# A spectral block on one core: a room of its own for the scaled sum, products of zeros in the first sequence, later weight conversions, and a later first inverse run

## Chip, cores and metric

One Trainium2 chip, one core of it. The metric is the device time of one launch, in microseconds: the median over runs, lower is better. Engines are named as in the profile: PE (TensorE, matmuls), PEld (its weight loads), DVE (VectorE), ACT (ScalarE), POOL (GpSimd), SP (SyncE, which issues all the DMAs here).

## What is computed

For 8 sequences x of 3136 rows and 256 columns, in fp32:

```python
X = rfft(x, axis=1)                          # attention part
Yr = Xr @ w_r - Xi @ w_i + b_r               # complex product, bias
Yi = Xr @ w_i + Xi @ w_r + b_i
Y  = softshrink(Yr, 0.01) + 1j * softshrink(Yi, 0.01)
y  = irfft(Y, n=3136, axis=1)

mixed = real(fft(fft(y, axis=1), axis=2))    # MLP part
u  = y + mixed
un = (u - mean(u)) / sqrt(var(u) + 1e-6)     # over the 256 columns
out = u + relu(un @ w_ch1) @ w_ch2           # 256 -> 1024 -> 256
```

## The kernel before

The 3136-point transform is split as 64 x 49. Each sequence b goes through three phases.

Phase 1 (p1) is the 64-point forward step (fwd tables, tile g_f1), folded by DVE and stored to DRAM (ad; for the first sequence four pieces aq, one per quarter). Phase 2 runs in four quarters q of eight frequencies u. p2_f2 loads af from DRAM, does the 49-point step in two bursts s (tile g_f2 in PSUM, L574) and copies the spectrum X out. p2_w multiplies by the weights wr, ws, wd (tile g_w; L637 for b = 0 with plain fp32, L178 with three products of split fp32 for the others), copies the common term to ks (L646), adds bias and shrinks on DVE (y, m, Y, L651 to L654). For q = 0 POOL builds yz, the first transposing step's input (L663, L664). p2_mix does the transform over the columns (g_mix, four steps per quarter) and stores md. p2_yt transposes Y (g_yt, four steps per quarter) and p2_g2 does the inverse 49-point step in two bursts (g_g2, L812), evicts it by ACT into bev tiles (L817) and stores them to bd (L820). Phase 3: p3_norm loads bf from bd and mt from md, does the inverse 64-point step (tile g_g1, quarters, L442), adds both into ut and takes the statistics; p3_tr transposes ut; p3_mlp1 and p3_mlp2 are the MLP in groups of up to four row blocks, h (L178) to hh and hl (L955, L956), then o (L178) over eight pieces f. At a group's end DVE makes t and a second product from the two o banks and rb, the inverse deviations (L987), adds them to total (L990) and stores the result.

The order is planned: each task is a generator that yields the time at which its next piece is due, in units of one sequence (T), a heap takes the earliest, and a scheduler orders each engine's instructions from that program order. An extra edge can be given by hand: issue_after(x) keeps instructions behind x on its engine, and after(key) holds a generator until another one has set the key. `late` in load_consts and weights is such an edge: the conversion comes behind the ks copy of quarter q of the first sequence, ks_in[0, q]. burst and quarters keep a run of small products together: ACT first copies two elements into the bank (the "held" copies, L443 and L461), so that the run starts when its last input is there.

SBUF tiles share rooms by tag, each with its number of buffers. What the change touches:

```python
# L295, L296: 128x512 zeros for keep_busy, in a buffer of "hl" (3)
# L816, L986: both in "bev", 2 buffers
bev = sb.tile([128, 512], F32, tag="bf" if odd else "bev", bufs=4 if odd else 2, name="bev")
t = rb if k else sb.tile([128, 512], F32, tag="bev", bufs=2, name="t")
# L912: first inverse run of b = 0, also behind the last product w_in[1, 0]
if b == 0 and ms[0] == 0:
    yield from after(("w", 1, 0))
```

keep_busy (L299) multiplies zeros on PE, 35 times behind the first forward step and 8 times behind the first quarter's weights. split_double (L189) turns the MLP weights, which arrive as 64-bit floats, into two fp32r halves: one ACT copy (L203), five DVE instructions (L204 to L212), for w1 also the subtraction of the column mean with two products on PE (L217, L218) and one DVE instruction (L220), then a cast on ACT (L222) and two DVE instructions (L223, L224). weights (L1009) does that in eight parts; the parts of w1 go two at a time. In PSUM there are four banks g, two h and two o.

Of the kernel before, what the change touches and what calls it, by code (L numbers as in the profile page):

```python
# [62 lines left out]
def tables():  # L63
# [26 lines left out]
    for u in range(U):  # L90
# [13 lines left out]
        else:  # L104
# [24 lines left out]
ROOMS = (("m", 1, 400), ("y1", 2, 400), ("eo", 2, 400), ("ks", 2, 400), ("xx", 2, 400),  # L129
         ("W0", 1, 2048), ("W1", 1, 2048), ("W2", 1, 2048), ("W3", 1, 2048), ("mq", 2, 2048),  # L130
         ("uth", 2, 1024), ("utl", 2, 1024), ("tot", 2, 1024), ("af", 2, 1024), ("mt", 2, 1024),
# [3 lines left out]
T = 10000  # L135
# [14 lines left out]
def spectral_block(ctx: ExitStack, tc: tile.TileContext, x, w_ri, b_ri, w1, w2,  # L150
# [89 lines left out]
    def load_consts():  # L240
        yield 0.97 * T
        w_v = w_ri.rearrange("a (k p) e -> a p k e", p=128)
        for name, tag in (("wr", "hh"), ("ws", "hh"), ("wd", "hl")):
            KF[name] = sb.tile([128, 2, D], F32, tag=tag, bufs=3, name=name + "f")
        behind("a0", out=KF["wr"], in_=w_v[0])
        wi = sb.tile([128, 2, D], F32, tag="mt", bufs=2, name="wi")
        behind("a0", out=wi, in_=w_v[1])

        for name, sign in (("ws", -1.0), ("wd", 1.0)):
            va.scalar_tensor_tensor(KF[name], wi, sign, KF["wr"], op0=ALU.mult, op1=ALU.subtract)  # L250
        yield 1.01 * T
        KF["cs"] = sb.tile([128, 2, 129], F32, tag="hl", bufs=3, name="csf")
        behind(1, out=KF["cs"], in_=c_cs)
        behind(1, out=fwd_f, in_=c_fwd)
        yield 1.6 * T
        nc.sync.dma_start(out=inv_f, in_=c_inv)
        late = ks_in[0, 2]
        for name in ("wr", "ws", "wd"):
            with tc.issue_after(late):
                split(name, KF[name])  # L260
            lo_v(K[name][1], KF[name], K[name][0])
        cs = K["cs"] = cp.tile([128, 2, 2, 128], F32R, name="cs")
        t = KF["cs"]
        with tc.issue_after(late):
            sc.copy(cs[:, :, 0], t[:, :, 0:128])
        lo_v(cs[:, :, 1], t[:, :, 0:128], cs[:, :, 0])
        with tc.issue_after(late):
            sc.copy(cs[:, 0, 1, 0:1], t[:, 0, 128:129])
# [24 lines left out]

    mlp_w = {}
    idle_f = sb.tile([128, 512], F32, tag="bev", bufs=2, name="idle_f")  # L295
    idle = sb.tile([128, 512], F32R, tag="hl", bufs=3, name="idle")  # L296
    va.memset(idle_f, 0.0)
    sc.copy(idle, idle_f)

    def keep_busy(last, n):  # L300

        g = gtile("g_idle")
        with tc.issue_after(last):
            for i in range(n):
                te.matmul(g, idle[:, :128], idle, start=True, stop=True)


    a_dram, b_dram, m_dram = {}, {}, {}
    af_ld, f2_in = {}, {}
# [148 lines left out]
    def burst(banks, lates, todo):  # L458


        held = [sc.copy(g[0:1, 0:2], late) for g, late in zip(banks, lates)]  # L461
        f, *args = todo[0]
        first = first_of[0] = f(*args).ins
        for h in held:
            tc.add_manual_dep(first, h.ins.name, mybir.DependencyInfo(mybir.DependencyClass.Sync, mybir.DependencyReason.DATA), reason="bank held")
        with tc.high_priority(), tc.issue_after(first):
            for f, *args in todo[1:]:
                f(*args)

    def p1(b):  # L470

# [80 lines left out]
    def p2_f2(b):  # L552


        for q in range(4):
            base, STEP, F2W, W0, WW, M0 = clock2(b, q)
            u0 = 8 * q
            yield base
            yield from after(("a", b, q) if b == 0 else ("a", b))
            if b == 0:  # L560
                X = sb.tile([128, 2, 2, 8, S], F32, tag=("Xh", "Xl")[q % 2], bufs=1, name="X")
                Xs = sb.tile([128, 2, 8, S], F32, tag=("Xsh", "Xsl")[q % 2], bufs=1, name="Xs")
                xt[b, q] = X, Xs
            else:
                xt[b, q] = Xh, Xl, Xsh, Xsl = x_tiles()
            afs, tfs = zip(*[rows_f2(b, q, s) for s in range(2)])

            for s in range(2):
                yield base + STEP * F2W * s / 2

                def one(i, t, k, j):
                    rows = slice(64 * i, 64 * i + N2)
                    first = t * D + k * 128 + j * 64
                    return te.matmul(banks[i][64 * j:64 * j + 64, k * 200 + t * S:k * 200 + t * S + S], afs[s][rows, first:first + 64],  # L574
                                     tfs[s][rows, t], start=True, stop=True)
                banks = [gtile("g_f2") for _ in range(2)]
                burst([banks[1]], [afs[s][64:65, 0:2]], [(one, i, t, k, j) for t in range(4) for k in range(2) for j in range(2) for i in range(2)])
                if b == 0 and q == 0:
                    f2_in[s] = first_of[0]
                    done.add(("f2", s))  # L580
                gv = [g[:, :400].rearrange("p (k t j) -> p k t j", k=2, t=4) for g in banks]

                def place(t, c=None):
                    return (t if c is None else t[:, :, c])[:, :, s::2]

                def evict(outs):
                    for c, o in enumerate(outs):
                        sc.copy(o, gv[c])
                    if q == 0 and s == 0:
                        for c, o in enumerate(outs):  # L590
                            sc.copy(o[:, :, 0, NM:], gv[1 - c][:, :, 0, NM:])
                if b == 0:
                    xv_ = [place(X, c) for c in range(2)]
                    evict(xv_)
                    va.tensor_add(place(Xs), *xv_)
                    continue
                lo_x = lo_v if b == 1 and q == 0 else lo_g
                xs = sb.tile([128, 2, 4, S], F32, tag="xs", bufs=1, name="xs")
                xh, xl = ([place(t, c) for c in range(2)] for t in (Xh, Xl))
                if s == 0:  # L600
                    xx = [sb.tile([128, 2, 4, S], F32, tag="xx", bufs=2, name="xx") for c in range(2)]
                    evict(xx)
                    for c in range(2):
                        sc.copy(xh[c], xx[c])  # L604
                        lo_x(xl[c], xx[c], xh[c])
                    va.tensor_add(xs, *xx)
                else:
                    im = sb.tile([128, 2, 4, S], F32, tag="im", bufs=1, name="im")
                    sc.copy(im, gv[1])
                    sc.copy(xh[0], gv[0])  # L610
                    va.tensor_add(xs, gv[0], im)
                    lo_v(xl[0], gv[0], xh[0])
                    sc.copy(xh[1], im)
                    lo_v(xl[1], im, xh[1])
                sc.copy(place(Xsh), xs)
                lo_x(place(Xsl), xs, place(Xsh))
# [49 lines left out]
    def p2_mix(b):  # L666
# [13 lines left out]
        for q in range(4):  # L680
# [40 lines left out]
            for ui in range(4):  # L721
# [3 lines left out]
                for e in range(2):  # L725
                    o = g[:100, e * 256:e * 256 + 256]
                    n = (129, 128)[e]
                    if b == 0:
                        te.matmul(o[:, :n], ef[:, e, 2 * ui:2 * ui + 2].rearrange("p s j -> p (s j)"), KF["cs"][:, e, :n], start=True, stop=True)
                    else:  # L730
                        cs = K["cs"][:, e].rearrange("p h e -> p (h e)")
                        te.matmul(o, eh[:, e, ui], cs, start=e == 0, stop=False)  # L732
                        n += n % 2
                        te.matmul(o[:, :n], el[:, e, ui], cs[:, :n], start=False, stop=e == 1)
                if b == 0:
                    sc.copy(mq[:, 1, ui], gv[:, :, 0])
                else:
                    sc.copy(low[:, :, 1:], gv[:, :, 1, 1:])
# [35 lines left out]
    def p2_yt(b):  # L774

        for q in range(4):
# [4 lines left out]
            for i in range(4):  # L781
# [7 lines left out]
                for v in range(2):  # L789
                    place = 2 * (2 * (i % 2) + v) + s  # L790
                    for o in range(2):
                        z = yz[:, o] if q == place == 0 else yw[:, o, place]
                        te.transpose(gt[:, (v * 2 + o) * 128:(v * 2 + o + 1) * 128], z.rearrange("p c w -> p (c w)"), ident)  # L793
                yf = sb.tile([128, 512], F32, tag=("yh", "yl")[i % 2], bufs=2, name="yf")
                sc.copy(yf, gt)
                yhl[b, q, i] = yf
# [1 line left out]
    def p2_g2(b):  # L798

        bd = b_dram[b] = dr.tile([2 * RT, U, D], F32, tag="bd", bufs=4, name=f"bd{b}")  # L800
        for q in range(4):
            base, STEP, F2W, W0, WW, M0 = clock2(b, q)
            for s in range(2):
# [5 lines left out]
                def one(h, i, v):  # L809
                    rows, j = slice(64 * i, 64 * i + 50), i ^ h  # L810
                    cols = slice(v * D, v * D + D)
                    return te.matmul(banks[i][64 * j:64 * j + 64, cols], tif[rows, 2 * h + v], ys[h][rows, cols], start=True, stop=True)  # L812
                burst([banks[1]], [ys[1][0:1, 0:2]], [(one, h, i, v) for v in range(2) for h in range(2) for i in range(2)])
                for i, g in enumerate(banks):
                    odd = b == 0 and i
                    bev = sb.tile([128, 512], F32, tag="bf" if odd else "bev", bufs=4 if odd else 2, name="bev")  # L816
# [14 lines left out]
    def p3_norm(b):  # L831
# [67 lines left out]
        for ms in pairs + [[NM - 1]] * (b % 2):  # L899
# [10 lines left out]
                finish(ms[0], 1)  # L910
                continue
            if b == 0 and ms[0] == 0:  # L912
                yield from after(("w", 1, 0))
            groups = [([gtile("g_g1") for _ in range(2)], [[bfs[r][64 * p:64 * p + 64] for r in range(2)] for p in range(2)], bfs[0][0:1, 0:2])
                      for mt, bfs in loads]
            quarters(inv_f, groups, w_in[1, 0] if b == 0 and ms[0] == 0 else None)
# [49 lines left out]
    def p3_mlp2(b):  # L966
        for gi, (g0, z) in enumerate(GROUPS[b % 2]):
# [15 lines left out]
            slot = (b % 2) * (NM - 1) + g0  # L983
            ts = []
            for k, o in enumerate(ops):
                t = rb if k else sb.tile([128, 512], F32, tag="bev", bufs=2, name="t")  # L986
                va.tensor_mul(t[:, :w], o, rb[:, :w])  # L987
                ts.append(t)
            for k, t in enumerate(ts):
# [3 lines left out]
    def weights():  # L993
# [14 lines left out]
        for k, (i, name, sl, src) in enumerate(todo):  # L1008
# [8 lines left out]
            if i:  # L1017
                split_double(name, h, l, [(sl, raws.pop(k))], False, ks_in[0, 2 + (k > 5)])
            elif k % 2:
                mark = (0, k // 2)  # L1020
                yield from after(("w",) + mark)
                split_double(name, h, l, [(todo[j][2], raws.pop(j)) for j in (k - 1, k)], True, ks_in[mark])

# [67 lines left out]
```

## Time and profile before

| | us |
|---|---|
| median of 3 runs | 1923.01 |
| the runs | 1922.76 to 1924.8 |
| the profiled execution, its own time | 1919.39 |
| its span, first to last instruction | 1917.6 |
| PE busy | 1802.4 |
| DVE busy | 1194.0 |
| mean granted PE clock | 0.958 |

The profile is one execution. A busy time is the sum of an engine's instructions; idle time is put down to what ended last before the next instruction began. Granted clock 1.00 is 2.4 GHz and 0.50 is 1.2 GHz; a value in between is a mean over the two.

### The profile page before, as it was taken

The page shows a single profiled execution, that of the slowest core. Times are in us where ns is not written, and L with a number is a line of the kernel's source. Part 1 is how long each engine was busy: PE and PEld are TensorE (multiplying, and loading weights), DVE is VectorE, ACT ScalarE, POOL GpSimd, SP SyncE. Part 2 cuts the span into 40 slices and gives each one's busy share as a digit, 9 for nine tenths or more (in the row PEclk, how much of TensorE's full clock was granted, in tenths as well). Part 3 has the DMA queues.
Part 4 walks back from the last instruction along what each step waited for, and adds up shares of the span by engine and source line. Part 5 has one row for each costly group of instructions (what it writes and reads, how often), then busy time and mean ns, then how long its engine had stood idle before and what let it go on. Part 6 is the DMA issues. An engine that isn't in the chain of part 4 may idle for free.

```text
span 1917.6 us, 37007 instructions
## 1 busy us (share of the span) xinstructions
PE 1802.4 (94%) x13447; PEld 1425.2 (74%) x13447; DVE 1194.0 (62%) x2754; ACT 788.5 (41%) x1957; POOL 539.9 (28%) x1005
## 2 busy tenths in 40 slices
PE   8786989999999799998999889998999999999998
PEld 4444767777777678777788677786778887777888
DVE  4665566666667557666757656665577576656553
ACT  2454544444444334444444443443544443432222
POOL 0001332332333323323324222333333342321220
PEclk9786989999999899999999899999999999999999
DMA  7656354555435534244443634336442452233210
GB/s 222 212 177 166 114 161 131 157 151 155 141 86 154 153 106 134 81 147 141 138 129 104 190 117 125 93 98 192 130 142 77 119 164 71 93 104 87 81 37 33
DMA packets 173014, 245.11 MB, mean 128 GB/s; under 512 B 30240, under 2 KB 115360, under 8 KB 172576
## 3 DMA queue, kind: packets, MB, share of 16 engines
q1 hardware_dynamic: 172832, 242.74, 43.2%
q8 instruction: 107, 1.75, 0.4%
q14 instruction: 75, 0.61, 0.1%
HBM read 135.66 MB, written 106.98 MB: 127 GB/s over the span
## 4 chain that ended last, share of the span: by engine, by line
PE 75%; DVE 8%; DMA 5%; SPq 3%; ACT 2%; issue 2%; POOL 1%; DVEq 0%; ACTq 0%; POOLq 0%
PE o L178 26%; PE h L178 25%; PE g_w L178 9%; PE g_g L812 3%; PE g_f L574 2%; PE g_yt L793 2%; DMA bd<-bev 2%; PE g_ut L937 2%; PE g_g L442 2%; PE g_f L442 1%; DMA af<-ad 1%; PE g_mix L732 1%; SPq L894 1%; DVE ut L839 1%; PE g_w L637 1%
## 5 line engine op out<-in xcount | busy, mean ns | idle before, releaser
L956 DVE SCALAR_TENSOR_TENSOR hl<-h,hh 128x512 fp32r<-128x512 f32 (+2 forms) x416 | 271.6, 655 | 361.9 <-ACT hh L955 350.4
L955 ACT ACTIVATE hh<-h 128x512 fp32r<-128x512 f32 (+2 forms) x416 | 238.3, 573 | 514.3 <-PE h L178 461.9
L178 PE MATMUL o<-hl,w2h 128*128 128x512 f32 (+2 forms) x832 | 335.2, 403 | 44.7 <-DVE t L987 29.6
L178 PE MATMUL h<-utl,w1h 128*128 128x512 f32 (+2 forms) x832 | 321.3, 386 | 4.0 <-DVE hl L956 4.0
L178 PE MATMUL o<-hh,w2l 128*128 128x512 f32 (+2 forms) x832 | 322.4, 388 | 0.0
L178 PE MATMUL o<-hh,w2h 128*128 128x512 f32 (+2 forms) x832 | 321.3, 386 | 0.0
L178 PE MATMUL h<-uth,w1l 128*128 128x512 f32 (+2 forms) x832 | 318.2, 382 | 0.0
L178 PE MATMUL h<-uth,w1h 128*128 128x512 f32 (+2 forms) x832 | 317.0, 381 | 0.0
L178 PEld LDWEIGHTS o<-hl,w2h 128*128 128x128 f32 x832 | 160.8, 193 | 105.1 <-DVE hl L956 37.5
L963 POOL TENSOR_TENSOR total<-uth,utl 128x256 f32<-128x256 f32 x200 | 145.5, 751 | 306.9 <-DMA out_dram<-total 158.5
L178 PEld LDWEIGHTS h<-utl,w1h 128*128 128x128 f32 x832 | 158.0, 190 | 37.2 <-DVE hl L956 6.8
L178 PEld LDWEIGHTS o<-hh,w2l 128*128 128x128 f32 x832 | 160.6, 193 | 28.5
L178 PEld LDWEIGHTS h<-uth,w1l 128*128 128x128 f32 x832 | 157.7, 190 | 29.7 <-issue 2.4
L178 PEld LDWEIGHTS o<-hh,w2h 128*128 128x128 f32 x832 | 161.2, 194 | 21.8 <-issue 0.8
L178 PEld LDWEIGHTS h<-uth,w1h 128*128 128x128 f32 x832 | 158.0, 190 | 25.6
L651 DVE SCALAR_TENSOR_TENSOR y<-g_w,small,ks 128x400 f32<-128x400 f32 x128 | 80.3, 628 | 71.7 <-PE g_w L178 46.2
L654 POOL TENSOR_TENSOR Y<-y,m 128x400 f32<-128x400 f32 x56 | 61.6, 1100 | 196.5 <-DVE m L653 172.9
L817 ACT COPY bev<-g_g 128x512 f32<-128x512 f32 x128 | 69.1, 589 | 69.9 <-PE g_g L812 69.6
L574 PEld LDWEIGHTS g_f<-tff,af 49*64 49x64 f32 x4096 | 74.1, 149 | 29.4 <-issue 10.1
L793 PE MATMUL g_yt<-ident,Y 128*128 128x128 f32 x496 | 87.7, 297 | 6.2 <-POOL Y L654 3.1
L574 PE MATMUL g_f<-tff,af 49*64 49x50 f32 x4096 | 82.2, 235 | 8.0 <-ACT g_f L461 2.5
L171 POOL TENSOR_TENSOR Xl<-xx,Xh 128x400 fp32r<-128x400 f32 x54 | 55.6, 1044 | 108.8 <-ACT Xh L604 108.5
(170 smaller groups left out, 3088.3 us busy)
## 6 DMA issues: line engine op xcount, KB each, us to landing
bd<-bev SPq DMA_DIRECT2D x256, 112.0 KB
bf<-bd SPq DMA_DIRECT2D x96, 256.0 KB
out_dram<-total SPq DMA_DIRECT2D x88, 256.0 KB
ad<-xf SPq DMA_DIRECT2D x84, 256.0 KB
md<-mq SPq DMA_DIRECT2D x112, 192.0 KB
af<-ad SPq DMA_DIRECT2D x112, 192.0 KB
xf<-in_x SPq DMA_DIRECT2D x39, 512.0 KB
mt<-md SPq DMA_DIRECT2D x192, 64.0 KB
```

Source lines behind the costliest of these rows:

```text
L171: gp.tensor_sub(out_, full, hi.bitcast(F32))
L178: last = te.matmul(o, l, r, start=start and i == 0, stop=stop and i == 2)
L442: return te.matmul(banks[i][64 * j:64 * j + 64], mat[rows, rows], movs[i][j], start=True, stop=True)
L574: return te.matmul(banks[i][64 * j:64 * j + 64, k * 200 + t * S:k * 200 + t * S + S], afs[s][rows, first:first + 64], tfs[s][rows, t], sta ...
L651: va.scalar_tensor_tensor(y1, gw, bias[:, c, o:o + 1], ks, op0=ALU.add, op1=ALU.add)
L654: (va if b == 0 or o == 0 else gp).tensor_sub(y[:, o, :, c, :], y1, m)
L793: te.transpose(gt[:, (v * 2 + o) * 128:(v * 2 + o + 1) * 128], z.rearrange("p c w -> p (c w)"), ident)
L812: return te.matmul(banks[i][64 * j:64 * j + 64, cols], tif[rows, 2 * h + v], ys[h][rows, cols], start=True, stop=True)
L817: sc.copy(bev, g)
L955: sc.activation(hh[:, :w], h[:, :w], AF.Relu)
L956: va.scalar_tensor_tensor(hl[:, :w], h[:, :w], 0.0, hh[:, :w].bitcast(F32), op0=ALU.max, op1=ALU.subtract)
L963: gp.tensor_add(total[:, k, cols], uth[:, k, cols].bitcast(F32), utl[:, k, cols].bitcast(F32))
```

## The change

A room t of one buffer is added. The zeros live in it first and every t afterwards; bev is left to the inverse step's evictions. A new helper, bridge, puts three products of zeros behind the last instruction of a step, for the first sequence only, into the two o banks: behind seven of its eight forward bursts (all but the first), its 16 mixing steps, its 16 transposing steps and its 8 inverse bursts. burst returns its last instruction for that. The splits of wr, ws and wd go behind the ks copies of quarters 0, 1 and 2 instead of all behind quarter 2's. The two halves of w1 are converted behind quarters 1 and 2 instead of 0 and 1. The first inverse run comes behind the second sequence's forward burst (q = 1, s = 1) instead of behind its first weights.

```diff
-         ("xf", 2, 1024), ..., ("ut", 4, 512), ("bev", 2, 512),
+         ("xf", 2, 1024), ..., ("ut", 4, 512), ("bev", 2, 512), ("t", 1, 512),
...
-        late = ks_in[0, 2]
-        for name in ("wr", "ws", "wd"):
+        for q, name in enumerate(("wr", "ws", "wd")):
+            late = ks_in[0, q]
             with tc.issue_after(late):
                 split(name, KF[name])
...
-    idle = sb.tile([128, 512], F32R, tag="hl", bufs=3, name="idle")
+    idle = sb.tile([128, 512], F32R, tag="t", bufs=1, name="idle")
...
+    def bridge(b, last, n=3):
+        if b == 0:
+            g = ps.tile([128, 512], F32, tag="o", bufs=2, name="g_fill")
+            with tc.issue_after(last):
+                for i in range(n):
+                    te.matmul(g, idle[:, :128], idle, start=True, stop=True)
@@ burst @@
-                f(*args)
+                last = f(*args).ins
+        return last
@@ p2_f2 @@
-                burst([banks[1]], ...)
+                last = burst([banks[1]], ...)
+                if b or q or s:
+                    bridge(b, last)
+                if b == 1 and q == 1 and s == 1:
+                    done.add(("f2", 1, 1))
@@ p2_mix, behind each ui, b == 0 @@
+                    bridge(b, last)
@@ p2_yt, behind each i, and in p2_g2, behind each s @@
+                bridge(b, last)
@@ p3_norm @@
             if b == 0 and ms[0] == 0:
-                yield from after(("w", 1, 0))
+                yield from after(("f2", 1, 1))
@@ p3_mlp2 @@
-                t = rb if k else sb.tile([128, 512], F32, tag="bev", bufs=2, name="t")
+                t = rb if k else sb.tile([128, 512], F32, tag="t", bufs=1, name="t")
@@ weights, first matrix @@
-                mark = (0, k // 2)
+                mark = (0, 1 + k // 2)
                 yield from after(("w",) + mark)
```

## Rows read from the trace of the kernel before

**Rows 1.** The page, part 1: busy us (share of the span) and instructions

```profile
PE 1802.4 (94%) x13447; PEld 1425.2 (74%) x13447; DVE 1194.0 (62%) x2754; ACT 788.5 (41%) x1957; POOL 539.9 (28%) x1005
```

**Rows 2.** Groups by line: busy us, mean ns | idle before, and its releasers

```profile
L178 PE MATMUL o<-hl,w2h 128*128 128x512 f32 (+2 forms) x832 | 335.2, 403 | 44.7 <-DVE t L987 29.6 <-DVE hl L956 14.6
...
L987 DVE TENSOR_TENSOR t<-o,rb 128x512 f32<-128x512 f32 (+2 forms) x52 | 34.2, 658 | 66.2 <-DMA bd<-bev 53.6 <-PE o L178 12.3
```

**Rows 3.** Waits of PE: us in total, times, longest

```profile
PE o L178 <- DVE t L987: 29.6, 9, 6.3
```

**Rows 4.** Timelines of SP, ACT, DVE, PE, one place: start, us, [idle before]

```profile
583.13 0.45 SPq L981 DMA_DIRECT2D rb<-rd  x1
...
622.07 1.07 ACT L817 COPY bev<-g_g 128x512 f32<-128x512 f32 x2 [0.54 <-PE g_g L812]
...
630.59 1.83 SPq L820 DMA_DIRECT2D bd<-bev  x4
...
633.42 0.69 DVE L987 TENSOR_TENSOR t<-o,rb 128x512 f32<-128x512 f32 x1 [8.52 <-DMA bd<-bev]
...
634.17 0.58 PE L178 MATMUL o<-hl,w2h 128*128 128x256 f32 x1 [5.98 <-DVE t L987]
```

**Rows 5.** Timeline of PE at the three other long waits

```profile
874.76 0.80 PE L178 MATMUL o<-hl,w2h 128*128 128x512 f32 x1 [6.18 <-DVE t L987]
...
1096.21 0.58 PE L178 MATMUL o<-hl,w2h 128*128 128x256 f32 x1 [4.35 <-DVE t L987]
...
1336.97 0.80 PE L178 MATMUL o<-hl,w2h 128*128 128x512 f32 x1 [6.35 <-DVE t L987]
```

**Rows 6.** Windows behind the four: length, busy PE PEld DVE ACT POOL, PEclk, DMA, GB/s

```profile
634.20:638.20 4.00, 4.00 (x20) 4.00 (x21) 3.75 (x8) 0.63 (x2) 1.19 (x4) 0.55 0.59 163
874.80:880.80 6.00, 6.00 (x17) 5.12 (x18) 4.56 (x14) 0.30 (x1) 2.63 (x9) 0.56 0.61 168
1096.20:1100.20 4.00, 3.99 (x19) 3.99 (x20) 3.75 (x9) 0.59 (x2) 1.19 (x4) 0.50 0.64 159
1337.00:1343.00 6.00, 6.00 (x20) 5.01 (x21) 5.16 (x15) 0.34 (x2) 2.63 (x9) 0.67 0.50 149
```

**Rows 7.** Windows of the first sequence's steps, same columns

```profile
53.00:165.00 112.00, 91.77 (x895) 55.76 (x895) 73.80 (x174) 57.05 (x153) 1.98 (x5) 0.73 0.60 185
...
40.00:56.00 16.00, 10.09 (x90) 6.05 (x88) 14.98 (x32) 3.82 (x9) 1.61 (x6) 0.83 0.75 201
...
97.00:107.80 10.80, 10.49 (x64) 5.27 (x68) 6.56 (x17) 5.44 (x17) 0.48 (x1) 1.00 0.66 205
107.80:127.00 19.20, 14.76 (x180) 9.38 (x180) 17.62 (x42) 12.47 (x33) 0.00 (x0) 0.70 0.61 184
127.00:143.00 16.00, 15.63 (x77) 8.72 (x77) 7.49 (x17) 6.39 (x14) 0.48 (x1) 0.82 0.51 146
```

**Rows 8.** Timelines of PE, ACT and DVE up to 56 us

```profile
17.59 8.53 PE L305 MATMUL g_idle<-idle 128*128 128x512 f32 x35
...
51.00 1.22 ACT L222 CAST w1h<-cv_w_ut 128x512 fp32r<-128x512 f32 x2 [7.17 <-DVE cv_w_ut L220]
...
53.13 0.69 PE L793 MATMUL g_yt<-ident,yz 128*128 128x128 f32 x2 [4.79 <-POOL yz L663]
...
53.88 1.28 DVE L224 TENSOR_TENSOR w1l<-cv_w_ut 128x512 fp32r<-128x512 f32 x2
```

**Rows 9.** Timelines of ACT, PE and SP around the first inverse run

```profile
179.05 0.15 ACT L443 COPY g_g<-bf 1x2 f32<-1x2 f32 x1 [10.32 <-DMA bf<-bd]
...
179.76 2.10 PE L442 MATMUL g_g<-bf,inv_f 64*64 64x512 f32 x8 [7.19 <-ACT ks L646]
...
180.55 0.43 SPq L546 DMA_DIRECT2D tff<-c_tf  x1
...
184.73 0.69 PE L793 MATMUL g_yt<-ident,yz 128*128 128x128 f32 x2 [2.87 <-POOL yz L663]
...
197.72 0.78 PE L178 MATMUL h<-utl,w1h 128*128 128x512 f32 x1
```

More of the change, by code (lines that the diff above doesn't have):

```diff
@@ L576, in p2_f2 @@
                 banks = [gtile("g_f2") for _ in range(2)]
-                burst([banks[1]], [afs[s][64:65, 0:2]], [(one, i, t, k, j) for t in range(4) for k in range(2) for j in range(2) for i in range(2)])
+                last = burst([banks[1]], [afs[s][64:65, 0:2]], [(one, i, t, k, j) for t in range(4) for k in range(2) for j in range(2) for i in range(2)])
                 if b == 0 and q == 0:
@@ L728, in p2_mix @@
                     if b == 0:
-                        te.matmul(o[:, :n], ef[:, e, 2 * ui:2 * ui + 2].rearrange("p s j -> p (s j)"), KF["cs"][:, e, :n], start=True, stop=True)
+                        last = te.matmul(o[:, :n], ef[:, e, 2 * ui:2 * ui + 2].rearrange("p s j -> p (s j)"), KF["cs"][:, e, :n], start=True, stop=True).ins
                     else:
@@ L792, in p2_yt @@
                         z = yz[:, o] if q == place == 0 else yw[:, o, place]
-                        te.transpose(gt[:, (v * 2 + o) * 128:(v * 2 + o + 1) * 128], z.rearrange("p c w -> p (c w)"), ident)
+                        last = te.transpose(gt[:, (v * 2 + o) * 128:(v * 2 + o + 1) * 128], z.rearrange("p c w -> p (c w)"), ident).ins
+                bridge(b, last)
                 yf = sb.tile([128, 512], F32, tag=("yh", "yl")[i % 2], bufs=2, name="yf")
@@ L812, in one @@
                     return te.matmul(banks[i][64 * j:64 * j + 64, cols], tif[rows, 2 * h + v], ys[h][rows, cols], start=True, stop=True)
-                burst([banks[1]], [ys[1][0:1, 0:2]], [(one, h, i, v) for v in range(2) for h in range(2) for i in range(2)])
+                last = burst([banks[1]], [ys[1][0:1, 0:2]], [(one, h, i, v) for v in range(2) for h in range(2) for i in range(2)])
+                bridge(b, last)
                 for i, g in enumerate(banks):
```

2 rows, old and new, of the table ROOMS are left out of this document.

## The prediction

> **What bounds the kernel now.** I read the page first. TensorE is busy for 94% of the span [rows 1], so what counts is where PE stands still and where it runs at the lower of its two clock levels. Of 115.2 us of idle PE (1917.6 less 1802.4), the groups by line put the largest single share on one line: the first matmul of an output accumulation, o<-hl,w2h, sat idle 44.7 us, 29.6 of them for t, the scaled sum of the group before [rows 2]. The same view shows what t itself waited for: 53.6 of its 66.2 us of idle DVE end with a DMA, bd<-bev [rows 2]. The waits by engine say that PE met this nine times, 6.3 us at most [rows 3].
>
> The timelines show one such place. ScalarE fills two bev buffers at 622.07; SyncE, busy with other loads, issues their stores only at 630.59; t has stood at the head of VectorE's queue for 8.52 us when it starts at 633.42; PE then starts o at 634.17 after 5.98 us of nothing [rows 4]. The scale vector rb had been issued at 583.13 [rows 4], so it is not what t waited for. bev has two buffers, and before the change t takes one of them, so t can't be written until a store that has nothing to do with it has landed. Four places carry 22.9 of the 29.6 us: 5.98, 6.18, 4.35 and 6.35 [rows 4, 5]. After each, PE runs for a few microseconds at or near the lower level (1.2 of 2.4 GHz): granted 0.55, 0.56, 0.50 and 0.67 over 4, 6, 4 and 6 us [rows 6].
>
> The other weak stretch is the start. From 53 to 165 us PE is busy 91.8 of 112 us at a granted clock of 0.73 [rows 7]; those are the steps of the first sequence, one after the other, and no MLP work is there yet to fill gaps.
>
> **The change, part by part.**
>
> *A room for t.* The wait for bd<-bev goes from all 52 t's. At the first place DVE was free at 624.9 (633.42 less 8.52) and PE at 628.2, so t and the second product, 0.69 us each, end 1.9 us before PE asks. What is late next is the ordinary order on DVE, which had nothing else ready there. I take the four waits whole, 22.9 us, and the time at the lower level behind them: a stretch w at clock c would have taken w times c, so 4 x 0.45 + 6 x 0.44 + 4 x 0.50 + 6 x 0.33 = 8.4 us. The five small waits (6.7 us together) I leave as they are, since DVE's own queue can keep t that late. Term: -31. Ends: -38 (the five go too) and -15 (half comes back as a wait for something else). Nothing new waits: the room is held by the zeros until the last bridge, before 165 us, and afterwards by one t per group, which its own addition frees right behind it. Moving the zeros out of hl turns that room's rotation by one; its first MLP use comes after 197 us [rows 9], when the tables that it follows there have long been split.
>
> *Products of zeros.* Behind 7 of the 8 forward bursts, 16 mixing steps, 16 transposing steps and 8 inverse bursts of the first sequence stand three 128x512 products each: 47 x 3 = 141. The 35 of the same shape already in the kernel took 8.53 us, 0.244 each [rows 8], so 34.4 us of PE at the full level, and twice that at the lower. They read SBUF, write the two o banks that nobody uses before the MLP, and cost no other engine anything. They pay in two ways. They lie in the 20.2 us in which PE has nothing to do there (112 less 91.8) and are free, and they may hold the clock: 91.8 us at 0.73 would be 67 at full, 24.8 less. Ends: -25 (all hidden, clock full) and +47 (34.4 / 0.73, none hidden, clock unchanged). The nearest row for the clock is 97 to 107.8 us, where the same short steps follow each other without a gap at a granted 1.00 [rows 7]; so I believe most of the clock, and a little over half of the bridges on the path: -22 + 19 = -3.
>
> A rule speaks against this part. The Trainium skill, "TensorE: Matmul & The Clock Gate", section "A second HAM failure mode: psum-queue depth-cycling", says that small idle spells between groups of matmuls, frequent enough, make the clock go to and fro between its levels and that the throughput pays between bursts. By it the bridges would be paid and the clock stay near 0.73, which makes this term up to +47; the row just named disagrees for dense steps, and no row here shows bridges between these steps.
>
> *First MLP weights a quarter later.* The first half of w1 (two parts) was converted from 40 to 56 us, when DVE was busy 14.98 of 16 us [rows 7]. The cast on ScalarE stood there 7.17 us for DVE, and PE waited 4.79 us for yz, whose inputs DVE was also making [rows 8]. Behind the cast in ScalarE's queue were the copies that open the next forward burst. All this can come about 5 us sooner. The second half moves into the third quarter. That is eight DVE instructions per part, sixteen in all, at up to 0.64 us (two took 1.28 [rows 8]): about 10 us, put into a stretch where DVE is busy 17.62 of 19.2 us; against it the splits of wr and ws leave that stretch (two DVE subtractions and two casts, about 1.3 us on each engine). Behind it DVE is busy only 7.49 of 16 us [rows 7], which covers half. Six mean products move along on PE, under what DVE does. On SyncE two loads of w1 slide behind the first conversion and two of w2 find their buffers later; all are wanted only from the third quarter on. Term: -5 + 5 = 0; ends -6 and +9.
>
> *First inverse run moved back.* At 179.05 ScalarE had stood 10.32 us before a copy that holds a bank for this run, until its rows had landed (bf<-bd); behind it in the queue was ks of the second sequence, and PE stood 7.19 us and then 2.87 us more for yz, which hangs on ks [rows 9]. Placed behind the second quarter's forward transform, the copy no longer blocks ks. So ks, yz and the transposes come some 7 us sooner. What this run gives to the first MLP group comes after the forward burst instead of before it, and that burst needs a table that SyncE issued only at 180.55 [rows 9]; so the MLP may gain less. The loads of this run keep their place on SyncE, and POOL gets nothing new. Term: -5; ends -10 (both idle spells) and +4 (the run waits for that burst, with the MLP behind it).
>
> Sum: -31 - 3 + 0 - 5 = -39 against the profiled execution's own 1919.4 us (span 1917.6 and 1.8 around it): 1880.4. The runs' median, 1923.0, is 3.6 above it, so I forecast 1884.
>
> **Rivals.**
>
> *Another wait takes t's place.* SyncE's queue runs late there, which was the reason for t's wait; with PE 6 us earlier at four places, tiles that come through the same queue may be what is late next. Half of the first term stays lost, and the start gives nothing: 1919.4 - 16 + 3.6 = 1907. For it: bd<-bev was held up for 7 us by other issues [rows 4]. Against it: only t is put down to that store. Chance 0.17.
>
> *The bridges hide and hold the clock.* Bridges -25, inverse -10, t -31, w1 0: 1919.4 - 66 + 3.6 = 1857. For it: PE's 20.2 us of idle. Against it: 34.4 us don't fit in 20.2, so the rest must be taken from waits that the higher clock doesn't shorten. Chance 0.12.
>
> *The bridges lie on the path and the clock stays.* Each bridge stands in PE's queue ahead of the next step, ready or not. At 0.73 that is 47 us against -31 - 5: slower by 11, 1934. It decides from about 40 us of path time on; the clock from 53 to 165 us would be near 0.73 and PE nearly without idle. This is what the skill's rule above would make of it; the row at 1.00 speaks against. Chance 0.05.
>
> *The room changes nothing.* If t waited for something else that came at the same time as the store, the nine waits stay and the rest comes out near even: within 0.2% of 1923. The early rb speaks against it [rows 4]. Chance 0.03.
>
> **How the numbers follow.** My forecast has 0.63. Faster by over 0.2% (3.8 us, about what a measurement of this kernel can tell from no change) holds in it and in the first two rivals: 0.92. Slower: 0.05. Same: 0.03. The range goes from 1860, short of the second rival, to 1910, over the first; it takes in the ends of t (-15) and of the inverse run, and leaves out most of the last two rivals and the far side of the second.
>
> **What would show it.** In the profile after: no t idle for bd<-bev, and o<-hl waiting for t less than 7 us in all; the four clock dips gone; PEclk in the first tenth of the span above 0.85 with PE's idle there down; no cast of w1h before 60 us, and a denser DVE in the third quarter; ks of the second sequence's first quarter right behind its product, and the first MLP product before 195 us rather than at 198. It would be wrong if o<-hl waits as long for hl or a DMA as it did for t, or if the first MLP product comes after 205 us.

## The result and the profile after

The changed kernel takes 1848.61 us (median; 1844.01 to 1850.72) against 1922.88 us in the same group of runs: ratio 0.9612 [0.9589, 0.9636]. It is faster by 74 us; 1884 was forecast, with 1860 as the low end. The profiled execution took 1847.56 us, its span is 1845.8 us.

From the page of the changed kernel, part 1 (busy us, share, instructions) and the shares of part 4 (the chain that ended last, by engine):

```profile
PE 1788.7 (97%) x13588; PEld 1418.8 (77%) x13588; DVE 1176.8 (64%) x2754; ACT 787.4 (43%) x1957; POOL 539.5 (29%) x1005
...
PE 86%; DVE 6%; SPq 2%; issue 2%; DMA 2%; POOL 1%; ACT 1%; DVEq 0%; POOLq 0%; ACTq 0%
```

PE has 141 instructions more than before [rows 1] and is still busy 13.7 us less; its idle time falls from 115.2 to 57.1 us (1845.8 less 1788.7).

Groups by line of the changed kernel (busy us, mean ns | idle before, releasers):

```profile
L178 PE MATMUL o<-hl,w2h 128*128 128x512 f32 (+2 forms) x832 | 329.0, 396 | 18.7 <-DVE hl L973 13.6 <-DVE mq L756 5.0
L315 PE MATMUL g_fill<-idle 128*128 128x512 f32 x141 | 47.6, 451 | 0.0
...
L1004 DVE TENSOR_TENSOR t<-o,rb 128x512 f32<-128x512 f32 (+2 forms) x52 | 33.9, 652 | 20.7 <-PE o L178 20.7
```

Beside [rows 2]: the 53.6 us in which t stood for bd<-bev are gone, and o<-hl waits for t nowhere. Its idle time falls from 44.7 to 18.7 us.

Windows of the changed kernel (length, busy of PE, PEld, DVE, ACT, POOL, PEclk, DMA, GB/s):

```profile
53.00:165.00 112.00, 100.78 (x891) 65.23 (x890) 79.01 (x182) 56.33 (x147) 1.92 (x4) 0.95 0.60 182
165.00:200.00 35.00, 27.54 (x258) 22.60 (x257) 21.02 (x52) 17.03 (x39) 12.89 (x27) 0.76 0.73 190
200.00:1845.80 1645.80, 1615.46 (x12063) 1302.37 (x12061) 1054.01 (x2468) 698.78 (x1732) 522.15 (x961) 1.00 0.44 125
```

And the last of these stretches in the kernel before:

```profile
200.00:1917.60 1717.60, 1648.76 (x12114) 1329.33 (x12112) 1079.23 (x2481) 705.36 (x1742) 524.22 (x964) 0.98 0.41 121
```

In the stretch of the first sequence's steps the granted clock went from 0.73 [rows 7] to 0.95. From 200 us on, PE's idle time fell from 68.8 to 30.3 us and its busy time from 1648.8 to 1615.5 (with 51 products fewer in that stretch, as the MLP began sooner). Timelines give the marks of the start: the first transpose of yz at 43.26 us (before: 53.13 [rows 8]), the first MLP product h at 190.46 (before: 197.72 [rows 9]).

So only 7 us of the gain were there when the MLP began, and 65 came behind it. That set the theories: the room is worth nearly all (R), or the products of zeros are worth 20 to 25 us by the clock (S), or the room is worth the forecast 31 and something else made the rest (F).

### The profile page after: what moved, and what is told of

Same layout as the page of the kernel before. It is cut to its first block, busy times and chain, and to the rows that moved or that the text cites. A ratio compares the mean times of both kernels' runs of the same rounds, so it can differ in the third digit from the quotient of the medians.

```text
span 1845.8 us, 37382 instructions
## 1 busy us (share of the span) xinstructions
PE 1788.7 (97%) x13588; PEld 1418.8 (77%) x13588; DVE 1176.8 (64%) x2754; ACT 787.4 (43%) x1957; POOL 539.5 (29%) x1005
## 4 chain that ended last, share of the span: by engine, by line
PE 86%; DVE 6%; SPq 2%; issue 2%; DMA 2%; POOL 1%; ACT 1%; DVEq 0%; POOLq 0%; ACTq 0%
PE o L178 28%; PE h L178 27%; PE g_w L178 10%; PE g_g L828 3%; PE g_f L584 3%; PE g_yt L808 3%; PE g_ut L954 2%; PE g_f L451 2%; PE g_g L451 2%; PE g_fill L315 2%; PE g_mix L746 2%; PE g_w L651 1%; DVE ut L856 1%; PE g_mix L748 1%; SPq L911 1%
## 5 line engine op out<-in xcount | busy, mean ns | idle before, releaser
L178 PE MATMUL o<-hl,w2h 128*128 128x512 f32 (+2 forms) x832 | 329.0, 396 | 18.7 <-DVE hl L973 13.6
L178 PE MATMUL o<-hh,w2l 128*128 128x512 f32 (+2 forms) x832 | 318.5, 383 | 0.0
L178 PE MATMUL h<-utl,w1h 128*128 128x512 f32 (+2 forms) x832 | 318.3, 383 | 0.1
L178 PE MATMUL o<-hh,w2h 128*128 128x512 f32 (+2 forms) x832 | 316.9, 381 | 0.0
L178 PE MATMUL h<-uth,w1h 128*128 128x512 f32 (+2 forms) x832 | 316.6, 381 | 0.0
L178 PE MATMUL h<-uth,w1l 128*128 128x512 f32 (+2 forms) x832 | 316.3, 380 | 0.0
L178 PEld LDWEIGHTS o<-hl,w2h 128*128 128x128 f32 x832 | 156.8, 188 | 75.5 <-DVE hl L973 43.0
L178 PEld LDWEIGHTS h<-utl,w1h 128*128 128x128 f32 x832 | 157.0, 189 | 31.2 <-DVE total L1007 1.6
L178 PEld LDWEIGHTS h<-uth,w1l 128*128 128x128 f32 x832 | 156.7, 188 | 29.2 <-issue 2.4
L178 PEld LDWEIGHTS o<-hh,w2l 128*128 128x128 f32 x832 | 157.0, 189 | 28.1 <-issue 0.8
L178 PEld LDWEIGHTS h<-uth,w1h 128*128 128x128 f32 x832 | 156.8, 188 | 27.6 <-issue 1.2
L178 PEld LDWEIGHTS o<-hh,w2h 128*128 128x128 f32 x832 | 157.1, 189 | 21.2
L584 PEld LDWEIGHTS g_f<-tff,af 49*64 49x64 f32 x4096 | 68.1, 138 | 24.9 <-issue 9.1
L808 PE MATMUL g_yt<-ident,Y 128*128 128x128 f32 x496 | 81.5, 281 | 5.3 <-DVE Y L668 2.0
L811 ACT COPY yf<-g_yt 128x512 f32<-128x512 f32 x128 | 75.5, 590 | 22.8 <-PE g_yt L808 22.0
```

The source lines that it names most:

```text
L178: last = te.matmul(o, l, r, start=start and i == 0, stop=stop and i == 2)
L808: last = te.transpose(gt[:, (v * 2 + o) * 128:(v * 2 + o + 1) * 128], z.rearrange("p c w -> p (c w)"), ident).ins
```

## Experiments

All ratios are to the kernel before, run on the same chip in the same group.

### The room of t

**Alone (e_room).** The kernel before, with

```diff
+ ("t", 1, 512)
- t = rb if k else sb.tile(..., tag="bev", bufs=2, name="t")
+ t = rb if k else sb.tile(..., tag="t", bufs=1, name="t")
```

> The kernel before with t in a room of its own, and nothing else of the change. Theory R (the room is nearly all of it: in the changed kernel the first inverse product starts only 7 us earlier than before, and the other 65 us come after it): 1855 to 1865 us, with the first 165 us as before (granted clock 0.73 from 53 to 165 us). Theory S (the products of zeros are worth 20 to 25 us, the room 45): 1873 to 1883 us. Theory F (the room is worth the 31 us that were forecast, the rest came from elsewhere): 1889 to 1895 us.

1860.38 us, 0.9688 [0.9667, 0.9709]: 60 us by the room alone, theory R. F falls. Its groups by line:

```profile
L178 PE MATMUL o<-hl,w2h 128*128 128x512 f32 (+2 forms) x832 | 329.3, 396 | 19.0 <-DVE hl L956 13.1 <-DVE mq L741 5.8
...
L987 DVE TENSOR_TENSOR t<-o,rb 128x512 f32<-128x512 f32 (+2 forms) x52 | 33.9, 653 | 21.8 <-PE o L178 18.5 <-DMA tif<-c_ti 3.4
```

No t waits for bd<-bev and no o for t. The 3.4 us are put down to the load of a table (tif).

**The change without it (e_tbev).** t back in bev.

```diff
- t = rb if k else sb.tile(..., tag="t", bufs=1, name="t")
+ t = rb if k else sb.tile(..., tag="bev", bufs=2, name="t")
```

> The changed kernel with t back in the room of the eviction tiles (the zeros keep their own room). Theory R: the waits on t come back with nearly all of the 74 us, 1905 to 1917 us. Theory S: 1890 to 1896 us. Theory F: 1877 to 1883 us.

1914.40 us, 0.9960 [0.9941, 0.9979]. The three other parts alone give 8 us, and t stood 55.2 us for bd<-bev again (53.6 before). R again.

**Four places, and all the others (e_four, e_rest).** The forecast put the whole term on four long waits and left the rest as it was. Two kernels split them, by the number of the group:

```diff
+ own = nt[0] in (10, 17, 23, 30)        # e_rest: not in
+ t = rb if k else sb.tile(..., tag="t" if own else "bev", bufs=1 if own else 2, name="t")
```

> The kernel before with a room of its own for t in only four of the 52 groups, those at 633, 874, 1095 and 1336 us, where t waited 7.1 to 8.5 us. Theory W (the waits add up and these four are worth the 31 us that were forecast; the 48 others make the other 29): 1887 to 1893 us. Theory G (a late t costs more than TensorE's own wait, and the four carry nearly all): 1860 to 1872 us. Theory N (the waits move on to the next t's): 1900 to 1920 us.

1882.26 us, 0.9801 [0.9786, 0.9816]: about 38 us by the ratio.

> The opposite: a room for t in the 48 other groups, and these four still among the eviction tiles. Theory W: 1886 to 1894 us. Theory G: 1905 to 1918 us. Theory N (a store is as late for the four as before, but nothing else is lost): 1865 to 1880 us.

1904.30 us, 0.9917 [0.9900, 0.9935]: about 16 us. Neither W nor G: the four are worth a little more than forecast, the others far more than nothing, and together they give some 54 of the room's 60.

e_four, groups by line and the window from 200 us on:

```profile
L178 PE MATMUL o<-hl,w2h 128*128 128x512 f32 (+2 forms) x832 | 333.6, 401 | 24.1 <-DVE t L991 13.8 <-DVE hl L956 8.1 <-DVE mq L741 1.6
...
L991 DVE TENSOR_TENSOR t<-o,rb 128x512 f32<-128x512 f32 (+2 forms) x52 | 34.1, 656 | 34.0 <-DMA bd<-bev 19.5 <-PE o L178 14.4
...
200.00:1881.60 1681.60, 1639.50 (x12116) 1321.85 (x12114) 1073.42 (x2481) 702.16 (x1742) 521.41 (x964) 0.99 0.42 123
```

e_room, the same window:

```profile
200.00:1860.80 1660.80, 1630.30 (x12134) 1315.97 (x12126) 1060.73 (x2484) 703.75 (x1745) 525.82 (x967) 0.99 0.43 125
```

Length less PE's busy time is its idle time: 68.8 us before, 42.1 in e_four, 30.5 in e_room. The four places took 26.7 us of idle time and 9.3 us of busy time (1648.8 to 1639.5, for the same work). The others took 11.6 and 9.2 us more. With the four cured, PE waits for t in seven places for 13.8 us, where the five small waits of before had 6.7: they don't stay as they are when PE comes sooner. Some of that is the same idle time under another name, though: over the same step the waits of o and h for hl fell from 18.6 to 8.1 us, and in e_room, where no o waits for t, they are 13.2 again, with 5.8 for mq. The sums of idle time don't depend on such names. Busy time times (1 - granted clock), summed over windows of 10 us from 200 us on, is 23.6 us before, 16.5 in e_four and 8.8 in e_room. By this estimate 7.0 of the 9.3 and 7.7 of the 9.2 us were time at the lower clock.

e_rest, groups by line:

```profile
L178 PE MATMUL o<-hl,w2h 128*128 128x512 f32 (+2 forms) x832 | 332.3, 400 | 39.9 <-DVE hl L956 15.3 <-DVE mq L741 12.4 <-DVE t L991 12.1
...
L991 DVE TENSOR_TENSOR t<-o,rb 128x512 f32<-128x512 f32 (+2 forms) x52 | 33.9, 651 | 48.2 <-DMA bd<-bev 31.9 <-PE o L178 16.4
```

All 31.9 us are the four t's (7.4 to 8.5 us each). PE's waits there stand half under t and half under mq: of two of them the profile names mq, which shares DVE's queue with the t in question. Read by the row for t alone, PE's loss is half of what it was.

**The same bytes as a third eviction buffer (e_bev3).** The kernel before, t still in bev.

```diff
- ("bev", 2, 512)
+ ("bev", 3, 512)
```

> The kernel before with a third buffer for the eviction tiles and t still among them: the same bytes as the room of t. Theory D (t lost time because it stood behind a store that was late; one more buffer puts that store one write further back): most of the waits on t go, 1858 to 1875 us. Theory E (only a room without any store helps): the store that t meets is as late as before, 1900 to 1920 us.

1858.17 us, 0.9682 [0.9650, 0.9714]: theory D. Not one t waits for a DMA:

```profile
L987 DVE TENSOR_TENSOR t<-o,rb 128x512 f32<-128x512 f32 (+2 forms) x52 | 33.8, 650 | 13.5 <-PE o L178 13.5
```

It needs no room without stores, only one more write between t and the store.

It also shows what the forecast had left out: PE's own order. In the kernel before, PE's timeline behind the last transposes at the first place reads

```profile
624.29 0.60 PE L793 MATMUL g_yt<-ident,Y 128*128 128x128 f32 x4
624.65 0.43 PE L178 MATMUL g_w<-Xsh,wrh 128*128 128x400 f32 x1
...
627.84 0.35 PE L178 MATMUL g_w<-Xh,wdl 128*128 128x400 f32 x1
```

and then the wait until 634.17 [rows 4]. In e_bev3:

```profile
613.85 0.60 PE L793 MATMUL g_yt<-ident,Y 128*128 128x128 f32 x4
614.20 0.37 PE L178 MATMUL o<-hl,w2h 128*128 128x256 f32 x1
```

Before, 18 products g_w stood between the transposes and o; now o follows at once, and the g_w are spread between later o's. The buffer count changes the order in which the instructions are laid down, so what a wait costs isn't only the idle time next to it. e_four has another order at this place too: six of the 18 products, then others, then the other twelve. No run has the order of before together with a t that is free, so how much of the 60 us, and of the 6 us by which e_four and e_rest don't add up, belongs to the order stays open.

### The products of zeros

**None (e_nobridge, and again as e_nob_again), one (e_n1), three (the change, again as e_again), six (e_n6).**

```diff
- if b == 0:
+ if b == 0 and n == 0:          # none
- def bridge(b, last, n=3):
+ def bridge(b, last, n=1):      # e_n6: n=6
```

> The changed kernel without the products of zeros behind the steps. Theory R (they are worth what the first inverse product gained, at most 7 us): 1851 to 1857 us. Theory S (they hold the clock and are worth 20 to 25 us): 1868 to 1875 us, and the granted clock from 53 to 165 us falls from 0.95 back to about 0.73. Theory F (3 us, as forecast): 1850 to 1853 us.

1843.52 us, 0.9592 [0.9566, 0.9618]. S falls: without the zeros the kernel isn't slower, and the granted clock from 53 to 165 us is 0.83, not 0.73.

> The changed kernel without the products of zeros, once more, as the measure for this group: 1840 to 1846 us.

1846.74 us, 0.9609 [0.9587, 0.9631].

> The changed kernel with one product of zeros at each place. Theory P (PE pays for each of them): between none and three, 1841 to 1847 us, the first product h near 186 to 188 us, PE's idle time up to 165 us between the two. Theory C (one is enough to hold the clock and fits into the gaps): below the kernel without any, 1833 to 1840 us.

1848.91 us, 0.9620 [0.9599, 0.9641]; first h at 186.86 us. Not theory C; P's range is missed by 2 us.

> The changed kernel as it is, once more, beside the next ones on the same chip: 1845 to 1851 us by every theory, as the measure for the other runs of this group.

1845.52 us, 0.9606 [0.9586, 0.9626]; first h at 188.62 us.

> The changed kernel with 6 products of zeros at each place and not 3. Theory P (the zeros stand in front of work that is ready; without them the kernel took 1843.5 us, so 3 cost about 5): another 5 to 12 us, 1853 to 1861 us, the first inverse product later than 190.5 us. Theory H (they lie in gaps): 1846 to 1850 us. Theory C (they are worth something by the clock): 1838 to 1845 us.

1868.36 us, 0.9722 [0.9703, 0.9742]; first h at 211.33 us. The direction of theory P, though twice as much.

At the end, none, one and three can't be told apart; six cost 23 us. At the first h the order is plain: 184.66 and 185.29 with none, 186.86 with one, 188.62 and 190.46 with three, 211.33 with six. Windows from the first yt to the second sequence's first weight product, L178 (the same work in each but for the zeros), and from there to the first h. In e_nobridge:

```profile
43.96:156.90 112.94, 88.79 (x900) 52.51 (x901) 79.31 (x186) 58.86 (x157) 1.90 (x4) 0.80 0.64 196
156.90:184.66 27.76, 20.31 (x216) 16.25 (x213) 15.14 (x39) 12.48 (x29) 9.15 (x15) 0.69 0.77 210
```

the changed kernel, and below that the zeros alone in it:

```profile
43.26:163.46 120.20, 108.98 (x1039) 71.39 (x1039) 80.52 (x186) 60.34 (x159) 1.92 (x4) 0.94 0.61 184
163.46:190.46 27.00, 19.54 (x214) 15.34 (x212) 15.21 (x39) 12.22 (x29) 9.47 (x16) 0.68 0.81 214
...
43.26:163.46 120.20, 46.43 (x138) 24.77 (x138) 0.94 0.61 184
```

and e_n6:

```profile
43.42:184.42 141.00, 137.49 (x1177) 95.39 (x1177) 80.90 (x186) 61.43 (x159) 1.91 (x4) 0.98 0.54 161
```

The zeros do raise the clock: 0.80, 0.94, 0.98. But many of them stand in PE's queue in front of work that is ready. The zeros take 46.4 us, the other work shrinks by 26.2 (88.8 to 108.98 - 46.43), idle time by 12.9 (24.15 to 11.22): +7.3 us. With six there is hardly any idle time left to lie in (3.5 us), the clock has nothing more to give, and the stretch grows by 20.8.

### The two moves at the start

**Casts back (e_w1back), and alone (e_w1only).**

```diff
+ late = ks_in[0, 2]
- for q, name in enumerate(("wr", "ws", "wd")):
-     late = ks_in[0, q]
+ for name in ("wr", "ws", "wd"):
- mark = (0, 1 + k // 2)
+ mark = (0, k // 2)
```

> The changed kernel with the casts of the MLP's first weights back a quarter earlier. If the forecast's zero holds: 1846 to 1852 us. If the earlier casts delay the first quarter's yt and the clear first quarter matters (yt stood at 43.3 us after, 53.1 before): 1854 to 1860 us, with yt near 53 us again. A third theory, that the casts in the third quarter cost more than they gave in the first: 1840 to 1845 us.

1856.65 us, 0.9673 [0.9650, 0.9696]. The first yt is at 54.91 us (43.26 in the change), the first h at 200.22 (190.46). The first quarter does matter. This edit and the next one move the splits of wr, ws and wd along, so that both moves are measured together.

> The kernel before with the casts of the MLP's first weights a quarter later, and nothing else of the change. By the forecast (0): 1918 to 1923 us. If the 8 us that they were worth in the changed kernel stand here too: 1910 to 1915 us, with the first quarter's yt near 43 us and not 53. If they are worth something only with the zeros behind them: 1917 to 1923 us although yt is earlier.

1917.88 us, 0.9979 [0.9964, 0.9995]. The first yt came at 45.01 us and the first h at 191.26 us, 6.5 sooner than before, but the end only some 4 us; in this profile t stood 61.5 us for bd<-bev and not 53.6. So with t behind the stores a better start may be partly lost again. It isn't shown, since the interval (1 to 7 us) takes in the 6.5. And the granted clock from 53 to 165 us is 0.82 here, without one of the new products of zeros.

**First inverse run free again (e_invback).**

```diff
- yield from after(("f2", 1, 1))
+ yield from after(("w", 1, 0))
```

> The changed kernel with the first inverse run free to start as soon as the second sequence's first products are done, as in the kernel before. By the forecast's term (5 us gained by holding it back): 1852 to 1856 us. If holding it back does nothing: 1846 to 1851 us. If it costs: 1838 to 1845 us.

1858.61 us, 0.9679 [0.9657, 0.9702], with the casts' move and the zeros in it: the forecast's direction, and more than twice its size, 13 us against the changed kernel in the same group (1845.52). PE's timeline in it:

```profile
177.71 2.10 PE L451 MATMUL g_g<-bf,inv_f 64*64 64x512 f32 x8 [7.82 <-DMA bf<-bd]
179.75 0.69 PE L808 MATMUL g_yt<-ident,yz 128*128 128x128 f32 x2
```

and in the changed kernel:

```profile
174.71 0.69 PE L808 MATMUL g_yt<-ident,yz 128*128 128x128 f32 x2 [4.52 <-POOL yz L677]
...
180.44 1.95 PE L451 MATMUL g_g<-bf,inv_f 64*64 64x512 f32 x8
```

Free, the run stands first in PE's queue and waits 7.8 us for its rows, with the transposes behind it; held back, the transposes are 5 us sooner and the run finds its rows there. The first h is at 196.11 us against 190.46 (188.62 in e_again).

### What paid, put together

Without zeros, the room's bytes as a third eviction buffer (e_nob_bev3); the same, and in the kernel with the room, with a subtraction moved from GpSimd to VectorE (e_nob_bev3_y, e_nob_y):

```diff
- (va if b == 0 or o == 0 else gp).tensor_sub(y...)
+ (va if b == 0 or o == 0 or q == 0 else gp).tensor_sub(y...)
```

The edit reaches further than the expectations say: q == 0 holds in the first quarter of every sequence, so 14 subtractions move, two in each of the seven later sequences (GpSimd has 42 of them left, of 56).

> Without the products of zeros, and in the second sequence's first quarter the subtraction that makes Y of the second half on VectorE and not on GpSimd (two spans of 1.0 to 1.2 us there, with PE waiting 4.5 us for yz behind them). If the end follows the first product h one for one: that comes 0.5 to 1.5 us sooner than without this step, and the end as much. If GpSimd's copies for yz set it anyway: no difference.

1839.14 us, 0.9578 [0.9555, 0.9600]; first h at 185.62 us, against 185.29 in e_nob_again.

> The parts that paid, with the same bytes: casts a quarter later, first inverse run held back, no products of zeros, and a third buffer for the eviction tiles in place of the room of t. If the room and the third buffer are worth the same on top of the other parts: 1840 to 1847 us. If the third buffer is worth the more that it showed alone (1858 against 1860): 1836 to 1842 us.

1842.57 us, 0.9599 [0.9585, 0.9612]: it can't be told from the room without zeros (0.9592 and 0.9609). In this trace two t's do meet a store again, for 1.2 us in all.

> The same, with the subtraction of the second sequence's first quarter on VectorE. If the 7 us that it was worth with the room of t are its own: 5 to 8 us under the run beside it. If they came of another instruction order by chance: within 3 us of it, to either side.

1841.02 us, 0.9583 [0.9562, 0.9604].

The subtraction's move brought 7.6 us in one pair and 1.6 in the other, and the first h came no sooner in either (in the second pair at 186.76 against 185.07 us). What it gave lies behind the first h: from there to the end the profiled executions need 1651.8 and 1652.2 us with the move, 1655.8 and 1655.4 without, which is 3 to 4 us in both pairs. The rest of the 7.6 isn't shown to be its own. The four kernels without zeros have ratios from 0.9578 to 0.9609, the changed kernel 0.9606 and 0.9612: without the 141 products no slower that these runs could tell, and at best some 0.3% faster.

### Start and rest

First h and span of the profiled executions, and the difference:

| kernel | first h, us | span, us | from first h to the end |
|---|---|---|---|
| before | 197.72 | 1917.6 | 1719.9 |
| e_tbev | 194.06 | 1914.7 | 1720.6 |
| e_w1only | 191.26 | 1916.9 | 1725.6 |
| e_rest | 199.70 | 1901.4 | 1701.7 |
| e_four | 198.50 | 1881.6 | 1683.1 |
| e_room | 200.95 | 1860.8 | 1659.9 |
| e_bev3 | 196.92 | 1855.3 | 1658.4 |
| e_invback | 196.11 | 1854.5 | 1658.4 |
| e_w1back | 200.22 | 1855.8 | 1655.6 |
| changed | 190.46 | 1845.8 | 1655.3 |
| e_nobridge | 184.66 | 1839.5 | 1654.8 |
| e_n6 | 211.33 | 1866.9 | 1655.6 |

Three kernels have t behind stores with two buffers, and need 1720 to 1726 us from the first h on. Seven don't, and need 1655 to 1660, whatever happened before; e_four and e_rest lie between. Among the four in which the first inverse run is held back (e_w1back, changed, e_nobridge, e_n6) the start moves the end one for one: the first h lies between 184.66 and 211.33 us, and the rest takes 1654.8 to 1655.6. The three in which it is free (e_room, e_bev3, e_invback) need 3 to 5 us more for that rest, and e_invback differs from the changed kernel by nothing else (1658.4 against 1655.3). So holding the run back gave something behind the first h as well; by what way stays open.

## Why the prediction was wrong

**The room: forecast -31, measured -60.** This is the step that failed, and it is where 29 of the missing 35 us are; the three other parts gave some 15 us on top of the room (0.9688 to 0.9612), where 8 were forecast. Its cause was right: t waited for a store that had nothing to do with it. The four long waits were sized well: 22.9 us idle and 8.4 of clock forecast, 26.7 and 9.3 measured (e_four against before). What failed is "The five small waits (6.7 us together) I leave as they are, since DVE's own queue can keep t that late". It doesn't: in e_room and in the change no o waits for t at all. With the four gone the small waits for t grew to 13.8 us (in part out of waits for hl), and taking t from them too brought 20.8 us (11.6 idle, 9.2 busy). The end of -38 for "the five go too" had the idle time of the trace before, but neither what the other waits came to once the four were gone nor the clock behind short waits. The sum of the 53.6 us in which t held up DVE was nearer to the truth than the 29.6 us that PE's rows put down to t: what queues behind t on DVE (hl, mq) passes the delay on under another name, as e_rest shows.

**Products of zeros: forecast -3, measured between nothing and +6.** Both halves of the working were off, in opposite ways. The clock did rise, and the steps' busy time fell by 26.2 us where 22 were expected; so the rival "The bridges lie on the path and the clock stays" falls on its second half. But the price of 0.244 us each came from a run of 35 in a row [rows 8]. In threes, 138 of them kept PE busy 46.4 us, 0.336 each (in e_n6, 276 took 78.5 us, 0.285 each). Only 12.9 us of idle time went, so 33.5 us of them lay on the path and not 19. And part of the clock would have come without them: 0.82 with the casts' move alone, 0.80 in e_nobridge's own stretch. The Trainium skill, "TensorE: Matmul & The Clock Gate", section "A second HAM failure mode: psum-queue depth-cycling", says of one kernel that small idle spells between groups of matmuls, frequent enough, made its clock swing between two levels. The traces agree in that the granted clock over the steps rose, 0.80, 0.94, 0.98, as their idle time fell, 24.15, 11.22, 3.5 us.

**First MLP weights: forecast 0, measured -10 at the first h.** The first quarter gave 11.6 us at yt (e_w1back against the change), not 5; of that, 9.8 were still there at the first h, so the third quarter took back about 2 us, not 5. At the end it is some 12 us (0.9673 against 0.9612 and 0.9606). DVE was busy 14.97 of 15 us from 106 to 121 us, as forecast, and of the 4.2 us for which PE stood there 3.7 were for DVE (Y and mq): what was too high was the price, not the reason.

**First inverse run: forecast -5, measured -5.7 at the first h and -13 at the end** (e_invback). The direction was right; that the first number lies so near owes something to luck. The forecast let the gain come through ks, which stood behind the run's held copy on ACT. In e_invback that copy still stood 8.78 us for the run's rows, but ks was ahead of it and no longer late (165.54 and 167.73 us). What stood in the way was the run's own first product in PE's queue. And the gain behind the first h was not in the forecast.

At the first h, room +3.2, casts -9.8, inverse -5.7 and zeros +5.8 make -6.5, and -7.3 was measured. That they meet proves no single term: two executions of the changed kernel differ by 1.8 us there (190.46 and 188.62), the second pair gives +3.3 for the zeros, and the four kernels that change only t's buffer lie between 196.92 and 200.95 us, with 197.72 before, so the room's +3.2 isn't shown. At the end, casts and inverse run taken back one at a time cost 12 and 13 us, together more than the 15 us that the three other parts give on top of the room; so the two overlap.

**The rivals.** "The bridges hide and hold the clock", at 1857, came nearest in time and was wrong in its cause: the zeros held the clock but didn't hide, and gave nothing. "Another wait takes t's place" falls: no wait of t on a DMA took it over, and of o<-hl's idle time only 13.6 us for hl (14.6 before) and 5.0 for mq are left. "The room changes nothing" falls with e_room.

**What would show it.** No idle time of t for bd<-bev, no wait of o on t, the higher clock at the start, the first h before 195 us: all came. The signs were right; that they came with a gain twice as large shows that none of them measured the size of the first term.

## What to carry to other kernels

A result that takes its buffer from the same rotation as tiles with stores is tied to those stores: look at what the write waits for, and count the idle time of the engine that is held up, all of it, since what stands behind it in its queue is late as well (here 53.6 us of it, and a gain of 60). One more buffer in the rotation did as much here as a separate room. Small waits are not to be left in the sum as they are: when the large ones went, they grew, and time at the lower clock came with them. Filler on a busy engine is to be priced in the lengths in which it will be issued, on the path first, and only then by the clock that it holds.

## Not expected of the hardware

A granted clock of 0.98 instead of 0.80 did not make up for the work that bought it (e_n6 against e_nobridge: 141.0 against 112.9 us for the same steps). And what the zeros did to the clock was gone behind PE's next long pause. The 27 us between the last zeros and the first h have the same mean with zeros before, 0.68, and without, 0.69, but not the same course. In the changed kernel:

```profile
167.00:172.00 5.00, 3.19 (x18) 2.85 (x16) 3.95 (x10) 0.49 (x1) 1.24 (x3) 1.00 0.95 227
172.00:177.00 5.00, 2.29 (x52) 1.97 (x54) 2.88 (x7) 2.64 (x7) 2.53 (x6) 0.63 0.72 231
177.00:182.00 5.00, 5.00 (x104) 3.28 (x99) 0.58 (x1) 4.09 (x10) 2.71 (x3) 0.50 0.83 229
```

PE stands 4.52 us for yz there, until 174.71 us; the granted clock is 1.00 ahead of that and 0.50, the lower level, behind it. In e_nobridge the stretch begins at 0.51, the clock is at 1.00 from 160.4 to 170.4 us, and behind a pause of 4.51 us (until 169.79) it is at 0.51 from 170.4 to 175.4.
